# Sliding-window attention backward: scores and their gradients as 32-row products, and background work in smaller pieces

## The chip, the cores and the metric

One core of a Trainium2 chip runs one program. The metric is device time of one execution in microseconds (us). Engines are named as the profile names them: PE is TensorE (PEld its weight loads), DVE is VectorE, ACT is ScalarE, POOL is GpSimd, SP issues most DMAs.

## What is computed

The forward is a gate between an attention block and a ReGLU block, and the kernel returns the output and the gradients to x and to all weights:

```
x = A_x                                     # 2048 x 512, bf16
g = sigmoid((x * gate_w).sum(-1))
q, k, v = split(x @ wqkv)                   # 32 heads of 16 channels
p = softmax(q k^T / 4, masked to 0 <= i - j < 256)
a = (p v) @ wo
b = (relu(x @ W_gate) * (x @ W_up)) @ W_down
out = g * a + (1 - g) * b
return out, vjp(out)(grad_out)              # to x, wqkv, wo, W_gate, W_up, W_down, gate_w
```

For the attention part this means, for every head, the scores S = k q^T, the exponentials P, the product dP = v dO^T, P*dP, and from P and P*dP the outputs and the gradients to q, k, v.

## The kernel before, in words

The work has three stages. The first (lines 189 to 456) does the ReGLU forward and its gradients. The second, the **attention stage** (lines 458 to 918), is where the change lies. The third (lines 920 on) is a loop over 16 row tiles that makes the output and the gradient to x.

**Channels and heads.** The 512 channels are cut into four chunks `c` of 128 channels, which are 8 heads. A chunk is four strips of 32 channels, and a strip holds two heads. Tokens are cut into 16 blocks of 128. A *group* is a chunk and 512 tokens (`tg`); `project_parts` (line 119) makes for a group Q, dO, K, V in transposed form (128 channels x 512 tokens), four accumulated products of 128x512 each (function `mm`), a DMA transpose of Q and dO (`tr_rows`) and a PE transpose of K and V (`tr_kv`). K and V are also kept in two masked copies, K0/K1 and V0/V1 (lines 153 to 160): `par` (line 440) zeroes the second or the first head of every strip.

**Units.** The attention stage is a list of 360 *units* (lines 627 to 641). A unit is a chunk, a query block `j`, a key block `kb` (j, j-1 or j-2; roles "d", "m" and "f") and a `half`, and it covers four of the eight heads: one from each strip. The loop from line 821 gives each unit one step `n`, and interleaves the stages of several units in it:

- `front` (643): one product `ST` of 128 rows by 512 columns. Its moving operand is `zt`, in which Q is spread out as a block diagonal: strip k stands in rows 32k to 32k+31 and columns 128k to 128k+127, and the rest is zero. Then exp on ACT to bf16 (`Pu`, or the first half of `PP`), and a triangular mask on POOL for roles "d" and "f".
- `front_dp` (663), at the end of the step: the like product `dPT` of V and the spread dO. `gradp` (671), one step later: P*dP on DVE. The spreading is done by four DMAs a group (`spread`, line 468); for the first group by copies (lines 145 to 151).
- `flip`: P and P*dP transposed, for later use as stationary operands; for units marked `dma` by a DMA transpose at step n+2, for the others at step n+3 by 8 PE transposes into PSUM (`pt`) and a copy out by ACT and DVE in turn.
- `rowsum` (679), at step n+3: 8 small products into `BA`. `small_ops` follow on DVE and POOL once for each j. `cd_piece` (480): 8 small products into `CD`.
- Background work: the parts of the next group's projection (`prq`), each part in one piece, and the weight gradients of the chunk before (`bgq`, `grad_parts`, line 557) in pieces of four products. A `credit` (lines 872 to 897) with fixed costs decides in which steps a piece goes out; while a piece with more to come is held open, no projection starts.

**PSUM**, eight banks: tag M has four one-bank buffers, shared by `ST`, `dPT`, projections and weight gradients; TR has two, for transposes; `CD` and `BA` have one each.

All engines run in the order in which the program issues to them, with semaphores between them. `manual_schedule` means that the order is the written one.

Of the kernel before, what the change touches and what calls it, by code (L numbers as in the profile page):

```python
# [22 lines left out]
def kernel(  # L23
# [89 lines left out]
    if True:  # L113
# [5 lines left out]
        def project_parts(c, tg):  # L119
# [3 lines left out]

            def mm(nm, which, eng):
                ps, tag, bufs, _ = pools["now"]
                pp = ps.tile([P, TGW], F32, tag=tag, bufs=bufs, name="pp")
                for cd in range(DC):
                    if which < 3:
                        nc.tensor.matmul(pp[:], lhsT=w_p[c][:, cd, which * P:(which + 1) * P], rhs=x_T[tg][:, cd, :],  # L129
                                         start=(cd == 0), stop=(cd == DC - 1))  # L130
                    else:
                        nc.tensor.matmul(pp[:], lhsT=w_p[c][:, cd, 3 * P:4 * P], rhs=da_T[tg][:, cd, :],
                                         start=(cd == 0), stop=(cd == DC - 1))
                if nm in ("Q", "dO"):
                    if nm == "Q":
                        t4["z"] = pjA.tile([P, 2, TGW], BF, tag="zT", name="zT")
                    dst = t4["z"][:, ("Q", "dO").index(nm), :]
                else:
                    dst = pjA.tile([P, TGW], BF, tag="T", bufs=2, name=f"{nm}T")[:]
# [5 lines left out]
                if nm in ("Q", "dO"):  # L145
                    if c == 0 and tg == 0:
                        w = ("Q", "dO").index(nm)
                        for k in range(NP):
                            rows = slice(32 * k, 32 * k + 32)
                            evac(zt[0][rows, w, :, k, :], dst[rows, :].rearrange("p (k q) -> p k q", k=TPG),  # L150
                                 (("dve", "act")[w] if k % 2 else "dve"))
                else:
# [9 lines left out]
            def tr(a_nm, b_nm):  # L162
                ps, tag, bufs, trt = pools["now"]
                pt = ps.tile([P, 2, TPG, P], BF, tag=trt, bufs=2, name="ptp")
                for a, nm in enumerate((a_nm, b_nm)):
                    for k in range(TPG):
                        nc.tensor.transpose(pt[:, a, k, :], t4[nm][:, k * P:(k + 1) * P], ident[:])
                return pt
# [7 lines left out]
            def tr_kv():  # L176
# [9 lines left out]
            return [lambda: mm("Q", 0, "dve"), lambda: mm("dO", 3, "dve"), tr_rows, lambda: mm("K", 1, "act"),  # L186
                    lambda: mm("V", 2, "act"), tr_kv]

    with ExitStack() as p1, tc.manual_schedule():
# [210 lines left out]
        pools["now"] = (ps1, "tr", 2, "tr")  # L400
# [3 lines left out]
        for n in range(N1 + 8):  # L404
# [38 lines left out]
            if t in (NT + 3, NT + 5):  # L443
                i = (t - NT - 3) // 2
                nc.gpsimd.memset(zt[i][:, 0, :, :, :], 0.0)
                nc.vector.memset(zt[i][:, 1, :, :, :], 0.0)
            if n == N1 - 2:
                first = project_parts(*groups[0])
            for _ in range({N1 + 1: 2, N1 + 2: 0}.get(n, 1)):
                if first:  # L450
                    first.pop(0)()
# [7 lines left out]
    if True:  # L459
# [7 lines left out]
        pools["now"] = (ps, "M", 4, "TR")  # L467
        def spread(gi, k):
            rows = slice(32 * k, 32 * k + 32)
            nc.sync.dma_start(zt[gi % ZB][rows, :, :, k, :],  # L470
                              proj[groups[gi]]["z"][rows, :, :].rearrange("p w (k q) -> p w k q", k=TPG))

# [7 lines left out]
        def cd_piece(c, kb, qb, half, last):  # L480
# [5 lines left out]
            for hh in range(HH):  # L486
                h = 2 * hh + half
# [52 lines left out]
        def load_wo():  # L540
            t = pjA.tile([P, 2, TGW], BF, tag="zT", name="wo_z")
# [15 lines left out]
        def grad_parts(c, rest=None):  # L557
# [13 lines left out]
            hold = {}  # L571

# [7 lines left out]
            def piece(part, t0, first, last):  # L580
                if first:
                    tag, bufs = ("TR", 2) if part == DC and rest is not None else ("M", 4)
                    hold[part] = ps.tile([P, 3, P] if part < DC else [P, D], F32, tag=tag, bufs=bufs, name="wps")
                wps = hold[part]
                for t in range(t0, t0 + 4):
                    go_, no_ = first and t == t0, last and t == t0 + 3
                    if part < DC:
                        nc.tensor.matmul(wps[:], lhsT=x_r[:, t, part * P:(part + 1) * P], rhs=sts[c][:, t, 0:3, :],  # L588
                                         start=go_, stop=no_)
                    else:  # L590
                        nc.tensor.matmul(wps[:], lhsT=sts[c][:, t, 3, :], rhs=rows[t], start=go_, stop=no_)
                if not last:
                    return None
                if part < DC:
                    ws = (gwp if rest is None else S2["t6"]).tile([P, 3, P], BF, tag="ws", bufs=2 if rest is None else 5, name="ws")
                    evac(ws[:], wps[:], "act" if rest is None or part % 2 else "dve")
                    return store(part, ws)
                if t0 + 4 < NT:
                    hold["half"] = gwp.tile([P, D], F32, tag="half", bufs=1, name="half")
                    evac(hold["half"][:], wps[:], "act")  # L600
# [4 lines left out]
                if "half" in hold:  # L605
                    nc.vector.tensor_tensor(out=ws[:], in0=hold["half"][:], in1=wps[:], op=ALU.add)
                else:
                    evac(ws[:], wps[:], "act")
# [10 lines left out]
            for part, a, b in parts:  # L619
                for t0 in range(a, b, 4):  # L620
                    out.append((lambda part=part, t0=t0, f=(t0 == a), l=(t0 + 4 == b): piece(part, t0, f, l), t0 + 4 < b))
# [6 lines left out]
        for c in range(DC):  # L628
            for j in range(NT):
                kbs = [k for k in (j - 1, j, j - 2) if k >= 0]  # L630
                for half in range(2):
                    order = kbs if half or len(kbs) < 3 else [kbs[0], kbs[2], kbs[1]]
                    for ki, kb in enumerate(order):
                        u = Unit()
                        u.c, u.j, u.kb, u.half = c, j, kb, half
                        u.first = ki == 0 and half == 0
                        u.last = ki == len(kbs) - 1 and half == 1
                        u.role = ("d", "m", "f")[j - kb]
                        u.dma = (u.role == "d" or (u.role == "m" and half == 0 and j % 2 == 1)) and (c < DC - 1 or j < NT - 2)
                        units.append(u)  # L640
        NU = len(units)

        def front(u):
            tg, jl = u.j // TPG, u.j % TPG
            z = zt[(u.c * NTG + tg) % ZB]
            KTt = proj[(u.c, u.kb // TPG)][f"K{u.half}"]
            ksl = slice((u.kb % TPG) * P, (u.kb % TPG + 1) * P)
            ST = ps.tile([P, HH, P], F32, tag="M", bufs=4, name="ST")
            nc.tensor.matmul(ST[:], lhsT=KTt[:, ksl], rhs=z[:, 0, jl, :, :], start=True, stop=True)  # L649
# [5 lines left out]
            nc.scalar.activation(u.Pu[:], ST[:], ACT.Exp)  # L655
# [7 lines left out]
        def front_dp(u):  # L663
            tg, jl = u.j // TPG, u.j % TPG
            z = zt[(u.c * NTG + tg) % ZB]
            VTt = proj[(u.c, u.kb // TPG)][f"V{u.half}"]
            ksl = slice((u.kb % TPG) * P, (u.kb % TPG + 1) * P)
            u.dPT = ps.tile([P, HH, P], F32, tag="M", bufs=4, name="dPT")
            nc.tensor.matmul(u.dPT[:], lhsT=VTt[:, ksl], rhs=z[:, 1, jl, :, :], start=True, stop=True)  # L669

        def gradp(u):
            if u.role != "d" and not u.dma:
                u.Pd = wk.tile([P, HH, P], BF, tag="Pd", bufs=3, name="Pd")
            nc.vector.tensor_tensor(out=u.Pd[:], in0=u.Pu[:], in1=u.dPT[:], op=ALU.mult)  # L674

        def rowsum(u):
# [4 lines left out]
            for hh in range(HH):  # L681
                h = 2 * hh + u.half
# [11 lines left out]
        def flip(u):  # L694
# [8 lines left out]
            pt = ps.tile([P, 2, HH, P], BF, tag="TR", name="pt")  # L703
# [96 lines left out]
        with tc.manual_schedule():  # L800
            ev = {}
            cdq = []
            bgq = []
            prq = []
            credit = 1.2
            SLOT = 1.5
            LAG = 3
            n = 0

# [3 lines left out]

            def background():
                f, more = bgq.pop(0)
                store = f()
                if store is not None:
                    ev.setdefault(n + 2, []).append(("dma", store))
                return more

            while n <= NU + LAG or ev or cdq or bgq:
# [5 lines left out]
                if u is not None:  # L827
# [3 lines left out]
                    if u.first and u.j % TPG == 0:  # L831
                        if gi + 1 < len(groups):
                            prq = project_parts(*groups[gi + 1])
                            due = n + sum(2 * min(3, j + 1) for j in range(u.j, u.j + TPG)) - 3
                            if gi + 2 == len(groups):
                                due -= 10
# [4 lines left out]
                    if u.first and u.j == TPG - 1 and u.c > 0:  # L841
                        bgq += ready
# [27 lines left out]
                if u is not None:  # L870
                    front_dp(u)
                credit += SLOT - 0.63 - (0.44 if LAG <= n < NU + LAG and not units[n - LAG].dma else 0.0)
                for _ in range(2 if len(cdq) > 6 or (len(cdq) > 1 and cdq[1][5] and cdq[1][0] <= n and cdq[1][2] < NT - 1) else 1):
                    if cdq and cdq[0][0] <= n:
                        cd_piece(*cdq.pop(0)[1:])
                        credit -= 0.2
                if n >= NU:
                    if bgq:
# [5 lines left out]
                elif held and credit > 0.3:  # L884
                    held = background()
                    credit -= 0.65
                elif prq and not held and (credit > 0.4 or due - n <= len(prq)):
                    credit -= (0.44, 0.86, 0.86, 0.1, 0.86, 0.86)[len(prq) - 1]
                    prq.pop(0)()
# [138 lines left out]
```

## Time and profile before

| | us |
|---|---|
| three runs, median (lowest to highest) | 970.55 (968.0 to 971.43) |
| profiled execution, its own time | 971.04 |
| its span in the profile | 969.0 |
| first and last start of `ST` (line 649) | 259.0 and 772.9 |
| PE busy, whole span | 938.9 |
| DVE, ACT, POOL busy, whole span | 501.5, 473.8, 488.4 |

The granted clock of the profiled execution was 0.994 on average. The attention stage lies between the two starts in the table: 513.9 us, or 1.43 us for one of the 360 units. "Busy" of PE is to be read with care: a matmul's row lasts until its modelled end, and the next one starts long before that. What a matmul costs PE is therefore the distance from its start to the next start, not the length of its row.

### The profile page before, as it was taken

The numbers are of one execution on the slowest core, as the hardware profiler recorded it, in microseconds if no ns is written. First come the engines' busy times: TensorE is split into PE (matmuls) and PEld (weight loads), VectorE is DVE, ScalarE is ACT, GpSimd is POOL, SyncE is SP. The second block draws the span as 40 slices with busy tenths as digits, with TensorE's granted clock in tenths as the row PEclk, the third lists the DMA queues.
The fourth block names the chain that finished last, engine by engine and source line by source line (L and its number), as shares of the span: only waits on it lengthen the run. The fifth ranks groups of instructions, "written<-read, shape, count | busy, mean of one in ns | idle before, by whom it ended". The sixth has DMA issues, their size and how long they took to land.

```text
span 969.0 us, 27638 instructions
## 1 busy us (share of the span) xinstructions
PE 938.9 (97%) x11281; PEld 598.3 (62%) x11281; DVE 501.5 (52%) x918; ACT 473.8 (49%) x811; POOL 488.4 (50%) x936
## 2 busy tenths in 40 slices
PE   7999999999999999999999999989999999999998
PEld 4556555656567777676776677756777754444443
DVE  4443323323377777666776667765667613223322
ACT  5422322222378777667776667766677720001001
POOL 2644345444177667666676556665657622121211
PEclk9999999999999999999999999998999999999999
DMA  9988899996667598985889857899999969866760
GB/s 291 185 201 206 218 218 210 220 196 174 143 114 122 100 160 155 154 146 100 145 126 189 138 103 139 127 162 175 160 141 229 185 184 260 194 171 165 183 155 28
DMA packets 447415, 161.64 MB, mean 167 GB/s; under 512 B 365784, under 2 KB 444984, under 8 KB 447288
## 3 DMA queue, kind: packets, MB, share of 16 engines
q1 hardware_dynamic: 424888, 136.80, 73.8%
q10 hardware_dynamic: 20592, 17.84, 6.1%
q0 software_dynamic: 1808, 5.24, 1.5%
q8 instruction: 88, 1.44, 0.7%
q14 instruction: 39, 0.32, 0.1%
HBM read 38.44 MB, written 38.41 MB: 79 GB/s over the span
## 4 chain that ended last, share of the span: by engine, by line
PE 82%; DMA 6%; POOL 4%; SPq 2%; DVE 2%; ACT 1%; issue 1%; ACTq 0%; POOLq 0%; DVEq 0%
PE pt L706 9%; PE dxps L970 8%; PE ST L649 7%; PE dPT L669 7%; PE wps L373 6%; PE wps L588 4%; PE dxps L991 4%; PE BA L683 4%; PE pp L129 4%; PE bps L941 4%; PE CD L488 4%; PE dhps L326 3%; PE ups L326 3%; PE dps L375 3%; PE gps L326 3%; PE CD L491 2%
## 5 line engine op out<-in xcount | busy, mean ns | idle before, releaser
L674 DVE TENSOR_TENSOR Pd<-Pu,dPT 128x512 bf16<-128x512 bf16 x201 | 136.6, 681 | 64.9 <-POOL Pu L660 53.5
L655 ACT ACTIVATE Pu<-ST 128x512 bf16<-128x512 f32 x201 | 121.6, 606 | 58.9 <-PE ST L649 57.3
L649 PE MATMUL ST<-z,K 128*128 128x512 bf16 x360 | 136.8, 380 | 4.0 <-DVE Pd L674 1.7
L669 PE MATMUL dPT<-z,V 128*128 128x512 bf16 x360 | 137.2, 381 | 1.3 <-DVE Pd L674 1.1
L674 DVE TENSOR_TENSOR PP<-PP,dPT 128x512 bf16<-128x512 bf16 x159 | 108.4, 682 | 41.0 <-POOL PP L657 38.1
L657 POOL TENSOR_SCALAR_AFFINE_SELECT PP<-PP 128x512 bf16<-128x512 bf16 x128 | 81.3, 635 | 79.5 <-ACT PP L655 78.8
L655 ACT ACTIVATE PP<-ST 128x512 bf16<-128x512 f32 x159 | 95.7, 602 | 51.7 <-PE ST L649 42.0
L340 POOL TENSOR_TENSOR hT<-rg,upm 128x512 bf16<-128x512 bf16 x44 | 52.2, 1186 | 123.9 <-DVE upm L338 98.4
L488 PE MATMUL CD<-rq,p 128*128 128x32 bf16 x1440 | 109.7, 177 | 0.8 <-ACT rows_st L494 0.5
L373 PE MATMUL wps<-dgu_r,x_r 128*128 128x256 bf16 x704 | 105.6, 272 | 4.9 <-DVE wst L74 4.9
L491 PEld LDWEIGHTS <-p 128*128 128x128 bf16 x1440 | 86.4, 96 | 35.9 <-issue 3.1
L72 ACT COPY p<-pt 128x1024 bf16<-128x1024 bf16 x103 | 105.1, 1020 | 5.2 <-PE pt L706 2.5
L491 PE MATMUL CD<-rq,p 128*128 128x16 bf16 x1440 | 106.7, 169 | 0.0
L488 PEld LDWEIGHTS <-p 128*128 128x128 bf16 x1440 | 99.0, 96 | 1.7 <-issue 1.5
L660 POOL TENSOR_SCALAR_AFFINE_SELECT Pu<-Pu 128x512 bf16<-128x512 bf16 x112 | 71.0, 634 | 41.8 <-ACT Pu L655 40.1
L373 PEld LDWEIGHTS <-x_r 128*128 128x128 bf16 x704 | 68.8, 98 | 36.7 <-issue 6.3
L948 ACT COPY a_sb<-aps 128x512 f32<-128x512 f32 x16 | 9.4, 585 | 145.8 <-issue 133.1
L706 PE MATMUL pt<-ident,Pd 128*128 128x128 bf16 x804 | 78.4, 220 | 0.0
L706 PE MATMUL pt<-ident,Pu 128*128 128x128 bf16 x804 | 77.7, 219 | 0.0
L74 DVE COPY p<-pt 128x1024 bf16<-128x1024 bf16 x102 | 69.5, 681 | 6.1 <-PE pt L706 5.4
L332 ACT ACTIVATE rg<-gps 128x512 bf16<-128x512 f32 x44 | 26.3, 598 | 91.0 <-PE gps L326 49.6
L683 PE MATMUL BA<-KV,Pu 128*128 128x33 bf16 x804 | 66.6, 178 | 4.1 <-ACT BAs L689 4.0
(158 smaller groups left out, 1998.7 us busy)
## 6 DMA issues: line engine op xcount, KB each, us to landing
dqkvo_d<-rows_st SPq DMA_DIRECT2D x7, 1024.0 KB, 5.7
dar<-da_d SPq DMA_DIRECT2D x28, 256.0 KB, 4.3
hT_d<-hT ACTq DMA_DIRECT2D x44, 128.0 KB, 2.4
dgT_d<-dgu ACTq DMA_DIRECT2D x44, 128.0 KB, 2.8
duT_d<-dgu ACTq DMA_DIRECT2D x44, 128.0 KB, 2.8
duT_g<-duT_d SPq DMA_DIRECT2D x8, 640.0 KB, 5.2
dgT_g<-dgT_d SPq DMA_DIRECT2D x7, 640.0 KB, 9.1
gt<-hT_d SPq DMA_DIRECT2D x7, 640.0 KB, 5.7
```

The costliest lines, as they stand in the source:

```text
L72: nc.scalar.copy(out, in_)
L326: nc.tensor.matmul(out[:], lhsT=w(c), rhs=x(c), start=(c == 0), stop=(c == DC - 1))
L373: nc.tensor.matmul(acc["w"][:, c, :], lhsT=x_r[:, t, c * P:(c + 1) * P], rhs=k.dgu_r[:, :, i, :], start=(go_ and c % 2 == 0), stop=no_, sk ...
L488: nc.tensor.matmul(cd[0][:, h, :], lhsT=p2[:, 0, hh, :], rhs=rq[:, h, 0:2 * Dh], start=cd[1], stop=True, skip_group_check=True)
L491: nc.tensor.matmul(cd[0][:, h, 0:Dh], lhsT=p2[:, 1, hh, :], rhs=rq[:, h, 2 * Dh:3 * Dh], start=False, stop=True, skip_group_check=True)
L649: nc.tensor.matmul(ST[:], lhsT=KTt[:, ksl], rhs=z[:, 0, jl, :, :], start=True, stop=True)
L655: nc.scalar.activation(u.Pu[:], ST[:], ACT.Exp)
L657: nc.gpsimd.affine_select(out=u.Pu[:], in_=u.Pu[:], compare_op=ALU.is_ge, fill=0.0, base=0, pattern=[[0, HH], [1, P]], channel_multiplier=-1)
L669: nc.tensor.matmul(u.dPT[:], lhsT=VTt[:, ksl], rhs=z[:, 1, jl, :, :], start=True, stop=True)
L674: nc.vector.tensor_tensor(out=u.Pd[:], in0=u.Pu[:], in1=u.dPT[:], op=ALU.mult)
L683: nc.tensor.matmul(BA[:, h, 0:33], lhsT=u.Pu[:, hh, :], rhs=kv[:, u.kb % TPG, h, 1:34], start=(u.first and hh == 0), stop=True, skip_group ...
L706: nc.tensor.transpose(pt[:, a, hh, :], src[:, hh, :], ident[:])
```

## The change

- A unit now covers two strips, both heads of each: `half` selects strips 0 and 1 or strips 2 and 3, and the six units of a query block are listed so that `half` alternates.
- `ST` and `dPT` become a tile `SD` of two banks. Each of the two products of 128x512 becomes four products with 32 rows (one strip, masked to one head) and 128 columns. `products(u, v)` issues at the start of step n the scores of unit n and the dP of unit n-1, eight products, in the order V0 V0 K0 K0 V1 V1 K1 K1. Because `half` alternates, the four of one round lie on four different strips and in four different banks.
- The spread copies of Q and dO, their DMAs (60), the first group's copies and the clearing of `zt` go away; the products read Q and dO as projected.
- PSUM: M has two buffers of two banks, for `SD` alone while units run. Projections and weight gradients move to tag "tr", which has two buffers and is shared with the transposes of `flip`.
- Projections go out in halves of two products, weight gradients in pieces of two. One list `bg` holds both; a budget spreads its cost evenly over the steps up to the end of the group (`until`), with planned costs of a step in `base`. The weight gradients of a chunk come in three lots.
- In the last chunk the last four query blocks (before: two) flip on PE alone, and so do three of the first units; 213 units flip on PE, before 205.

```diff
+            def mm_part(nm, which, cds):
+                if 0 in cds:
+                    ps, tag, bufs = pools["now"]
+                    acc4[nm] = ps.tile([P, TGW], F32, tag=tag, bufs=bufs, name="pp")
+                src = x_T[tg] if which < 3 else da_T[tg]
+                for cd in cds:
+                    nc.tensor.matmul(acc4[nm][:], lhsT=w_p[c][:, cd, which * P:(which + 1) * P], rhs=src[:, cd, :],
+                                     start=(cd == 0), stop=(cd == DC - 1))
...
-                if nm in ("Q", "dO"):
-                    if c == 0 and tg == 0:
-                        w = ("Q", "dO").index(nm)
-                        for k in range(NP):
-                            rows = slice(32 * k, 32 * k + 32)
-                            evac(zt[0][rows, w, :, k, :], dst[rows, :].rearrange("p (k q) -> p k q", k=TPG),
-                                 (("dve", "act")[w] if k % 2 else "dve"))
...
+            for nm, which, eng in (("Q", 0, "dve"), ("dO", 3, "dve"), ("K", 1, "act"), ("V", 2, "act")):
+                out.append((0.432, lambda nm=nm, which=which: mm_part(nm, which, range(DC // 2)), True))
+                out.append((0.432, lambda nm=nm, which=which, eng=eng: mm(nm, which, eng), False))
+            out.insert(4, (0.0, tr_rows, False))
+            out.append((0.45, tr_kv, False))
...
-        pools["now"] = (ps, "M", 4, "TR")
-        def spread(gi, k):
-            rows = slice(32 * k, 32 * k + 32)
-            nc.sync.dma_start(zt[gi % ZB][rows, :, :, k, :],
-                              proj[groups[gi]]["z"][rows, :, :].rearrange("p w (k q) -> p w k q", k=TPG))
+        pools["now"] = (ps, "tr", 2)
...
+            step = 2 if rest is None else 4
...
+                elif first:
+                    hold[part] = ps.tile([P, 3, P] if part < DC else [P, D], F32, tag="tr", bufs=2, name="wps")[:]
...
+                order = [(j - 1, 0), (j - 2, 1), (j, 0), (j - 1, 1), (j - 2, 0), (j, 1)]
...
+                    u.dma = (u.role == "d" or (u.role == "m" and half == 0 and j % 2 == 1)) and (c < DC - 1 or j < NT - 4)
+                    if c == 0 and j < 2 and half == 0:
+                        u.dma = False
...
+        def score(u, nm, w, at, par):
+            tg, jl = u.j // TPG, u.j % TPG
+            lhs = proj[(u.c, u.kb // TPG)][f"{nm}{par}"]
+            z = proj[(u.c, tg)]["z"]
+            ksl = slice((u.kb % TPG) * P, (u.kb % TPG + 1) * P)
+            return [lambda i=i: nc.tensor.matmul(u.SD[:, i, at + par, :], lhsT=lhs[32 * (2 * u.half + i):32 * (2 * u.half + i) + 32, ksl],
+                                                 rhs=z[32 * (2 * u.half + i):32 * (2 * u.half + i) + 32, w, jl * P:(jl + 1) * P],
+                                                 start=True, stop=True, skip_group_check=True) for i in range(2)]
+
+        def products(u, v):
+            if u is not None:
+                u.SD = ps.tile([P, 2, 4, P], F32, tag="M", bufs=2, name="SD")
+            for par in range(2):
+                for f in (score(v, "V", 1, 2, par) if v is not None else []) + (score(u, "K", 0, 0, par) if u is not None else []):
+                    f()
...
-            nc.tensor.matmul(ST[:], lhsT=KTt[:, ksl], rhs=z[:, 0, jl, :, :], start=True, stop=True)
...
-            nc.scalar.activation(u.Pu[:], ST[:], ACT.Exp)
+            nc.scalar.activation(u.Pu[:].rearrange("p (i r) q -> p i (r q)", i=2), u.SD[:, :, 0:2, :].rearrange("p i r q -> p i (r q)"), ACT.Exp)
...
-            nc.tensor.matmul(u.dPT[:], lhsT=VTt[:, ksl], rhs=z[:, 1, jl, :, :], start=True, stop=True)
...
-            nc.vector.tensor_tensor(out=u.Pd[:], in0=u.Pu[:], in1=u.dPT[:], op=ALU.mult)
+            flat = lambda a: a.rearrange("p (i r) q -> p i (r q)", i=2)
+            nc.vector.tensor_tensor(out=flat(u.Pd[:]), in0=flat(u.Pu[:]), in1=u.SD[:, :, 2:4, :].rearrange("p i r q -> p i (r q)"), op=ALU.mult)
...
+            pt = ps.tile([P, 2, HH, P], BF, tag="tr", bufs=2, name="pt")
...
+            def base(m):
+                b = 0.205
+                if m <= NU:
+                    b += 0.33
+                if LAG <= m < NU + LAG:
+                    b += 0.205 if units[m - LAG].dma else 0.65
+                return b
...
+                        until = n + sum(2 * min(3, j + 1) for j in range(u.j, u.j + TPG)) - 3
+                        if u.j == TPG and u.c > 0:
+                            jobs = ready
+                        for _ in range((0, 2, 2, 2)[u.j // TPG] if u.c < DC - 1 else (0, 3, 3, 0)[u.j // TPG]):
+                            if jobs:
+                                bg += jobs.pop(0)
...
+                if n <= NU:
+                    products(u, units[n - 1] if n >= 1 else None)
...
+                elif bg:
+                    left = max(1, until - n)
+                    credit += (sum(base(m) for m in range(n, n + left)) + sum(b[0] for b in bg)) / left - base(n)
+                    while bg and credit >= 0.5 * bg[0][0]:
+                        credit -= bg[0][0]
+                        held = background()
+                    credit = max(-1.0, min(1.0, credit))
```

## The prediction, as put on record before the changed kernel ran

> **What bounds the kernel now.** I read the page's busy shares first, then busy time by stretches, then the timeline of a few steps.
>
> ```profile
> PE 938.9 (97%) x11281; PEld 598.3 (62%) x11281; DVE 501.5 (52%) x918; ACT 473.8 (49%) x811; POOL 488.4 (50%) x936
> ...
> L649 PE MATMUL ST<-z,K 128*128 128x512 bf16 x360 | 136.8, 380 | 4.0 <-DVE Pd L674 1.7
> L669 PE MATMUL dPT<-z,V 128*128 128x512 bf16 x360 | 137.2, 381 | 1.3 <-DVE Pd L674 1.1
> ```
>
> PE is always busy, and its `ST` and `dPT` hardly ever waited (4.0 and 1.3 us). But busy is row length, so I take prices from distances between starts:
>
> ```profile
> 500.36 0.38 PE L669 MATMUL dPT<-z,V 128*128 128x512 bf16 x1
> ...
> 500.57 0.18 PE L488 MATMUL CD<-rq,p 128*128 128x32 bf16 x1
> ...
> 500.60 0.17 PE L491 MATMUL CD<-rq,p 128*128 128x16 bf16 x1
> ...
> 502.24 0.38 PE L706 MATMUL pt<-ident,Pu 128*128 128x128 bf16 x4
> ...
> 502.46 0.39 PE L706 MATMUL pt<-ident,Pd 128*128 128x128 bf16 x4
> ```
>
> A 512-column product costs 0.21 us (500.36 to 500.57), though its row is 0.38 long; a 16- or 32-column one with its own weights 0.0256 (500.57 to 500.60; the 16 of two CD pieces elsewhere take 0.41); a 128-column one 0.055 (four in 0.22). A 384-column one is taken in proportion, 0.16.
>
> The attention stage by these prices, with the counts of the built program: ST and dPT 720 x 0.2133 = 154; BA and CD 5760 x 0.0256 = 147; flips 1640 x 0.0548 = 90; projections 240 x 0.2133 plus 7 of transposes = 58; weight gradients of three chunks 192 x 0.16 + 48 x 0.2133 = 41. Sum 490 of the 514 us between the first and the last ST. **The stage is bound by PE's issue**; 24 us are gaps, most of them BA behind the copy of the former BA on ACT, and starts of chunks. From the starts of ST, chunks last 118, 129, 128 and 139 us; the first is shorter, as it has no weight gradients beside it.
>
> The next limit shows in one unit, whose ST started at 501.82:
>
> ```profile
> 502.26 0.60 ACT L655 ACTIVATE PP<-ST 128x512 bf16<-128x512 f32 x1
> ...
> 502.94 0.63 POOL L657 TENSOR_SCALAR_AFFINE_SELECT PP<-PP 128x512 bf16<-128x512 bf16 x1 [0.32 <-ACT PP L655]
> ...
> 503.12 1.04 ACT L72 COPY p<-pt 128x1024 bf16<-128x1024 bf16 x1
> ...
> 503.60 0.69 DVE L674 TENSOR_TENSOR PP<-PP,dPT 128x512 bf16<-128x512 bf16 x1 [0.27 <-POOL PP L657]
> ```
>
> Scores to P*dP take 2.47 us (501.82 to 504.29), over two steps of 1.2 to 1.5. The four M buffers let PE run ahead of that. In full stretches ACT and DVE are busy some 75% (here, of 24 us):
>
> ```profile
> 331.00:355.00 24.00, 23.89 (x430) 17.18 (x428) 18.07 (x32) 17.95 (x31) 17.33 (x40) 1.00 0.90 161
> ```
>
> (PE, PEld, DVE, ACT, POOL, clock, share of DMA time, GB/s.)
>
> **The change, part by part.**
>
> *The eight products.* They replace 0.427 us a unit. No row shows 32-row products, nor four strips at once. From below: 8 x 0.0256 = 0.205, the rate of eight other products with eight weight loads (BA), if streaming is hidden wholly by overlap. From above: without overlap 8 x 0.0548 = 0.44; if besides PE has to empty at each change between 128-row and 32-row products, a short row lasts 0.170 where the next starts after 0.026, so 0.145 more, twice a step: 0.73. I take 0.32, the middle of the first two rows, since both are rows of 8 weight loads and 8 products, and only the overlap lies between them. Saving: 360 x (0.427 - 0.32) = 38 us of PE.
>
> The Trainium skill (TensorE: Matmul & The Clock Gate, Part 3: Packing small matmuls) gives 3.07 times for four 32-row products of 512 columns; by that a round of four would be about 0.07 us, an estimate, and the unit would stand at the bound from below. No run here shows it yet.
>
> *Flips.* Eight more on PE: 8 x 0.44 = 3.5 us. DMA transposes 155 to 147, and 60 spread DMAs of 64 KB less on SP's queue; nothing waits for SP at length, so nothing is gained (they would cost if DMA, at 0.5 to 1.1 of its time, were the bound; it gets lighter). Clearing `zt` (two memsets each on POOL and DVE) lay beside a full PE in the first stage: 0. ACT's exp and DVE's product keep 512 elements a partition: 0.6 and 0.68, as before.
>
> *New waits, first kind: "tr".* While a projection or a weight gradient is held open in one of the two "tr" buffers, two flips in following steps share the other. In the built order 69 of 210 steps with a flip wait so, 39 for an ACT copy, 30 for DVE. Timetable of such a pair, from the step's start: products to 0.32, BA 0.53, flip 0.97, its end seen at 1.2; ACT copies 1.2 to 2.22. The next flip would be due 0.53 into the next step, at 2.03 if this one lasted 1.5: it waits 0.25. Behind it on PE stand CD, the background piece and the next products. DVE copies 1.3 to 2.0: about no wait. Sum 39 x 0.25 = 10 us.
>
> *New waits, second kind: two SD buffers.* In the built program the first V product of a step waits for ACT (the exp of unit n-1, which reads the same tile), and the first K product for DVE (the P*dP of unit n-2). So PE can no longer run ahead. Two loops follow. Exp: 0.06 to see it + (0.32 - 0.04) issue + 0.22 for the last product + 0.06 + 0.60 = 1.22 a step. P*dP for a masked unit: 0.56 to exp + 0.60 + 0.08 + 0.635 + 0.06 + 0.68 + 0.06 less 0.08 (V goes ahead of K) = 2.6 for two steps; for role "m" 1.16 a step; over m, f, d on average 1.25. ACT's 1.02 us copies stand in both loops at times. So **a step can't be shorter than about 1.25**, whatever PE has to do.
>
> *Sum by chunk.* PE's work beside the products, from the built order, is 0.79 a step in chunk 0 and 0.98 in chunks 1 to 3 (0.96, 1.18 and 0.79 in the thirds of the last).
> - Chunk 0: 0.79 + 0.32 = 1.11, so the loops decide: 90 x 1.25 + 5 of gaps as before = 117, before 118: -1.
> - Chunks 1 and 2: (0.98 + 0.32) x 90 = 117, + 3 old gaps, + 3.5 tr waits, + 1.5 for short steps under 1.25: 125, before 129 and 128: -7 in all.
> - Chunk 3: thirds at 1.28, 1.50 and 1.25: 121, + 13 old gaps (start, clock at 0.86 for a while), + 2: 136, before 139: -3.
>
> Together -11, and 2 more where even spreading shortens the old waits of BA: **-13 us**. First and last stage are left alone. The profiled execution took 971.04 (span 969.0 and 2.0 around it), 0.5 above the median of the runs. **Forecast 958 us.** The gain of 38 on PE is mostly given back: 21 us of the stage becomes PE waiting for ACT and DVE.
>
> **Rivals.**
> 1. *Full overlap.* Products at 0.205. For it: nothing but the issue rate of BA. The loops shrink to about 1.15 to 1.2. Chunk 0 113, 1 and 2 118 each, 3 129: -36, **935 us**.
> 2. *No overlap.* Products at 0.44; the strips don't help. For it: the transposes' rows. The exp loop becomes 1.34, chunks 126, 134, 134, 144: +24, **995 us**. This is the change not doing what it says.
> 3. *PE empties at each change of form (the slower side).* Two changes a step at 0.145, with full overlap inside: 0.205 + 0.29 = 0.495. Steps: 0.9 + 0.495 = 1.4 in chunk 0, 1.47 in chunks 1 and 2, thirds of 1.45, 1.68 and 1.4. Chunks 131, 138.5, 138.5, 151: +45, **1016 us**; with products one by one besides, +130. It decides against the change from about 0.36 a unit on, that is 0.08 a switch. For it: rows of 0.17 with a next start after 0.026 show how much is in flight. Against it: nothing in this trace, which holds one form only.
>    The Trainium skill (TensorEngine Tiling (Array Packing), Key Properties) says it outright: "Changing tiling mode (not just tile) drains the TensorE". It states no price; no run shown so far has a change of mode.
> 4. *Loops longer than I think.* Products at 0.32, but ACT's copies (1.02, some 107) push exp back 0.2 to 0.35 each in most cases: +25 on my sum, **983 us**. For it: ACT and DVE at 75%, and PE without its lead. Against it: such a push hurts only where the step is short, and the budget fills steps evenly.
>
> **How the numbers follow.** Forecast case 0.42, rival 1 0.20, rival 2 0.12, rival 3 0.16, rival 4 0.10. The forecast case runs from about 940 to 972, so some of it is no change or a little slower. A measurement of this kernel can tell 0.3% (3 us) from no change. Faster: 0.20 + 0.35 = 0.55; within 0.3%: 0.05; slower: 0.02 + 0.38 = 0.40. Range: from 925 (rival 1 with shorter loops) to 1020 (rival 3), leaving out a tenth on each side. Of the faster cases alone, 928 to 965.
>
> **What would show it.** In the changed profile: the distance from the first V product to the first BA of a step is the price of the products (0.32; 0.2 and 0.44 to 0.5 for the rivals); if PE empties, the gap stands before the first V and before the first BA, with no releaser named. PE's idle time should now name ACT (exp) before V and DVE (P*dP) before K, and flips should wait for copies `p<-pt`. Steps of chunk 0 should be near 1.25 us. I am wrong if the products cost under 0.25 or over 0.4, or if steps are far from the longer of PE's work and 1.25.

## The result, and the profile after

The changed kernel takes **1012.08 us** (median of 4 runs, 1009.82 to 1013.17) against 970.99 for the kernel before: a ratio of 1.0427, 95% interval 1.0397 to 1.0456. It is 4.3% slower; the forecast was 958. The profiled execution took 1013.17, with a span of 1011.2, 42.2 more than before (969.0).

First the place: busy time over the attention stage, of the kernel before and of the changed one (the columns are the stretch, its length, busy us of PE, PEld, DVE, ACT and POOL, granted clock, share of DMA time, GB/s).

```profile
259.00:773.00 514.00, 500.27 (x8527) 356.46 (x8528) 354.15 (x644) 367.19 (x628) 333.45 (x772) 0.99 0.84 145
```

```profile
262.00:813.00 551.00, 492.70 (x10671) 357.13 (x10744) 365.48 (x648) 373.17 (x632) 336.78 (x771) 0.96 0.77 128
...
382.00:430.00 48.00, 42.17 (x924) 30.61 (x927) 33.09 (x60) 32.51 (x56) 32.54 (x77) 0.89 0.80 118
430.00:502.00 72.00, 64.87 (x1400) 46.02 (x1409) 45.91 (x82) 47.95 (x83) 42.40 (x95) 1.00 0.85 142
```

The stage is 37 us longer (first to last score product 261.9 to 813.0, before 259.0 to 772.9); the other 5 lie ahead of it and behind it. PE is busy 89% of it in place of 97% (a little more in truth: the page has 126 fewer rows of PE than of its weight loads). DVE has 11 us more to do and ACT 6, which fills neither, and the clock has fallen.

Then the products. PE's rows of one step in the changed kernel's timeline:

```profile
499.97 0.23 PE L649 MATMUL SD<-zT,V 32*128 32x128 bf16 x2
499.98 0.23 PE L649 MATMUL SD<-zT,K 32*128 32x128 bf16 x2
500.04 0.22 PE L649 MATMUL SD<-zT,V 32*128 32x128 bf16 x2
500.04 0.22 PE L649 MATMUL SD<-zT,K 32*128 32x128 bf16 x2
500.19 0.19 PE L687 MATMUL BA<-KV,PP 128*128 128x33 bf16 x1
```

Four products on four strips start within 0.01 us, the second round 0.07 later, and BA 0.15 after that. Before the first V, PE's start is later than the price of the product ahead of it by 0.076 (median, behind CD) or 0.10 (behind a projection). Sum **0.31 us** a step, where 0.427 stood. So PE's own work on these products did shrink, by 42 us.

What grew is shown by the page's groups (idle time before them, and what ended it, at the end):

```profile
L678 DVE TENSOR_TENSOR Pd<-Pu,SD 128x512 bf16<-128x512 bf16 x203 | 139.1, 685 | 71.2 <-PE SD L649 46.9
L666 ACT ACTIVATE Pu<-SD 128x512 bf16<-128x512 f32 x203 | 121.8, 600 | 88.6 <-PE SD L649 83.6
L649 PE MATMUL SD<-zT,V 32*128 32x128 bf16 x1440 | 120.4, 225 | 27.4 <-ACT PP L666 19.5
...
L649 PE MATMUL SD<-zT,K 32*128 32x128 bf16 x1440 | 105.2, 223 | 19.1 <-DVE PP L678 10.9
```

V waits for ACT, K waits for DVE, and ACT and DVE in turn wait for PE (`SD`): a ring, in which everybody waits for somebody and nobody is full. The page counts idle time only from the modelled end of the last row; from the start and the price of the last product (and 0.08 for the change of form) I count **33 us in which V waits for an exp that ended later, and 38.5 in which K waits for P*dP**. In about 170 of the 360 steps PE waits over 0.05 us for one of them or for both. One such wait in the changed kernel's timeline:

```profile
349.81 0.59 DVE L157 TENSOR_SCALAR V<-VT,par 128x512 bf16<-128x512 bf16 x1
...
350.04 0.23 PE L649 MATMUL SD<-zT,V 32*128 32x128 bf16 x2
350.33 0.68 DVE L678 TENSOR_TENSOR PP<-PP,SD 128x512 bf16<-128x512 bf16 x1
...
351.06 0.23 PE L649 MATMUL SD<-zT,K 32*128 32x128 bf16 x2 [0.79 <-DVE PP L678]
```

DVE is in the masked copies of a projection when P*dP falls due, PE has issued two V products and stands for a microsecond: the scores of unit n need the buffer that P*dP of unit n-2 still reads.

### The profile page after: what moved, and what is told of

Same layout as the page of the kernel before. It is cut to its first block, busy times and chain, and to the rows that moved or that the text cites. A ratio compares the mean times of both kernels' runs of the same rounds, so it can differ in the third digit from the quotient of the medians.

```text
span 1011.2 us, 31916 instructions
## 1 busy us (share of the span) xinstructions
PE 932.8 (92%) x13379; PEld 601.3 (59%) x13505; DVE 508.6 (50%) x914; ACT 478.7 (47%) x813; POOL 488.9 (48%) x934
## 5 line engine op out<-in xcount | busy, mean ns | idle before, releaser
L678 DVE TENSOR_TENSOR Pd<-Pu,SD 128x512 bf16<-128x512 bf16 x203 | 139.1, 685 | 71.2 <-PE SD L649 46.9
L666 ACT ACTIVATE Pu<-SD 128x512 bf16<-128x512 f32 x203 | 121.8, 600 | 88.6 <-PE SD L649 83.6
L649 PE MATMUL SD<-zT,V 32*128 32x128 bf16 x1440 | 120.4, 225 | 27.4 <-ACT PP L666 19.5
L678 DVE TENSOR_TENSOR PP<-PP,SD 128x512 bf16<-128x512 bf16 x157 | 107.5, 685 | 68.4 <-POOL PP L668 46.4
L649 PE MATMUL SD<-zT,K 32*128 32x128 bf16 x1440 | 105.2, 223 | 19.1 <-DVE PP L678 10.9
L649 PEld LDWEIGHTS <-V 32*128 32x128 bf16 x1440 | 56.8, 92 | 101.3 <-issue 92.9
L666 ACT ACTIVATE PP<-SD 128x512 bf16<-128x512 f32 x157 | 94.5, 602 | 46.0 <-PE SD L649 44.3
L481 PEld LDWEIGHTS <-p 128*128 128x128 bf16 x1440 | 94.0, 97 | 0.3
L484 PEld LDWEIGHTS <-p 128*128 128x128 bf16 x1440 | 87.4, 97 | 0.8 <-issue 0.5
L710 PE MATMUL pt<-ident,Pu 128*128 128x128 bf16 x812 | 81.4, 225 | 4.1 <-ACT p L72 2.3
L710 PE MATMUL pt<-ident,Pd 128*128 128x128 bf16 x812 | 82.7, 227 | 0.0
```

Of the source, the lines that this page charges most:

```text
L481: nc.tensor.matmul(cd[0][:, h, :], lhsT=p2[:, 0, hh, :], rhs=rq[:, h, 0:2 * Dh], start=cd[1], stop=True, skip_group_check=True)
L484: nc.tensor.matmul(cd[0][:, h, 0:Dh], lhsT=p2[:, 1, hh, :], rhs=rq[:, h, 2 * Dh:3 * Dh], start=False, stop=True, skip_group_check=True)
L649: return [lambda i=i: nc.tensor.matmul(u.SD[:, i, at + par, :], lhsT=lhs[32 * (2 * u.half + i):32 * (2 * u.half + i) + 32, ksl], rhs=z[32 ...
L666: nc.scalar.activation(u.Pu[:].rearrange("p (i r) q -> p i (r q)", i=2), u.SD[:, :, 0:2, :].rearrange("p i r q -> p i (r q)"), ACT.Exp)
L678: nc.vector.tensor_tensor(out=flat(u.Pd[:]), in0=flat(u.Pu[:]), in1=u.SD[:, :, 2:4, :].rearrange("p i r q -> p i (r q)"), op=ALU.mult)
L710: nc.tensor.transpose(pt[:, a, hh, :], src[:, hh, :], ident[:])
```

## The experiments

Theory A: the loss is PE waiting in two loops (exp to V, P*dP to K), since each unit's S and dP tie up a pair of banks and there are two pairs. Theory B: the loss lies in what PE itself has to issue (narrow products, changes of form, small pieces, shared "tr" buffers).

Ratios are to the kernel before, which ran beside each experiment; there its medians were 968.1 to 968.5 us, and 970.99 beside the changed kernel. A difference in us between two of the other kernels is therefore good to about 3 us.

**Wide products back.** `ST` and `dPT`, the spread copies, units of one head from each strip and four one-bank M buffers as in the kernel before, in the changed kernel's loop (the lines on the products alone):

```diff
-            u.SD = ps.tile([P, 2, 4, P], F32, tag="M", bufs=2, name="SD")
...
+            ST = ps.tile([P, HH, P], F32, tag="M", bufs=4, name="ST")
+            nc.tensor.matmul(ST[:], lhsT=KTt[:, ksl], rhs=z[:, 0, jl, :, :], start=True, stop=True)
...
+            nc.tensor.matmul(u.dPT[:], lhsT=VTt[:, ksl], rhs=z[:, 1, jl, :, :], start=True, stop=True)
```

> Part alone: the products are the old 128-row, 512-column ones again (spread copies, four one-bank buffers, dP at the end of its step), while the small pieces, the even budget, the shared tr buffers and the new unit order stay. Theory A (the loss is PE waiting for exp and for P*dP, because the narrow products tie S and dP of a unit to one pair of banks and leave two such pairs): those waits go, PE runs ahead again, only the tr waits (10 us) and eight more flips (3.5 us) stay, less what even spreading saves: about 980 us, from 968 to 988. Theory B (the loss comes from the pieces, the tr buffers and the budget): stays at 1000 us or more.

Measured: 984.25 us (ratio to the kernel before 1.0164, 1.0135 to 1.0192), clock 0.998. As A says: some 28 of the 41 us came with the narrow products and their paired banks, though these products are cheaper for PE. In the trace the gap ahead of flips is 13.8 us and PE's waits for exp or P*dP are all but gone; the longest entries of PE's waits in the stage are:

```profile
PE BA L698 <- ACT BAs L704: 7.2, 16, 1.1
PE pt L721 <- DVE p L74: 3.2, 5, 1.2
PE pt L721 <- ACT p L72: 3.0, 10, 0.5
```

**All eight products of one unit.**

```diff
-                for f in (score(v, "V", 1, 2, par) if v is not None else []) + (score(u, "K", 0, 0, par) if u is not None else []):
+                for f in (score(u, "K", 0, 0, par) + score(u, "V", 1, 2, par)) if u is not None else []:
```

> The eight products of a step all belong to the same unit (K0 K0 V0 V0 K1 K1 V1 V1): dP no longer comes a step later, so no product waits for the exp of the unit before; only two strips overlap at a time, in two banks. Theory A: the 33 us in which V waited for exp vanish, the wait for P*dP (38 us) shrinks by about half, since role m ends 0.7 us sooner; inside the products PE pays some 0.08 a step more (29 us): 975 to 995 us. Theory B (PE's own price of the narrow products is what costs): dearer by those 29 us, 1030 to 1045 us.

Measured: 1038.76 us (1.0726, 1.0689 to 1.0764). A's range is missed by 44 us, and the time is B's. The trace shows both sides. V waits for no exp any more, as it should. But the four rounds of two (starts 350.67, 350.73, 350.78, 350.84, BA at 351.00) and their entry cost 0.42 a step, 38 us more in all than the changed kernel's 0.31; K's wait rises instead of halving, to about 46 us by the gaps ahead of the first product; and the clock is 0.946. From 1012, less 33 for V's wait, with 38 for the products and 8 for K's wait, that gives 1025 us. For the other 14 the clock is enough: the stage has the half clock for 109 us in place of 48, and the distances between PE's rows there exceed their full-clock prices by 31 us in place of 11. So this time doesn't decide between A and B: V's wait went as A says, the products became a third dearer, and the clock fell.

**Masks left out.** The two `affine_select` of `front` are dropped.

> Leaves out the triangular masks on POOL, so the weights of masked pairs are not zeroed; all else as in the changed kernel. Exp to P*dP gets about 0.75 us shorter for two units in three. Theory A with the loop through P*dP binding: K's waits (38 us) mostly go, 975 to 990 us. Theory A with the loop through exp binding: V's waits stay, 1000 to 1008 us. Theory B: 1012 us, unchanged.

Measured: 999.85 us (1.036, 1.030 to 1.0421; the four runs lie between 997.38 and 1009.44). K's wait falls from 38.5 to 28 us, V's stays at 33. The gain is 12 us by the medians and about 6 by the ratios, whose intervals overlap, so its size is uncertain. It lies at the edge of A's second answer: the loop through P*dP counts, but cutting 0.75 us from it frees only about a quarter of K's waits.

**All copies of flips on DVE.**

```diff
-            eng = ("act", "dve")[copier["i"] % 2]
+            eng = "dve"
```

> All 213 copies of flips go to DVE, where one takes 0.68 us in place of 1.01 on ACT. Theory A, exp loop: exp is no longer late behind a copy, V's waits fall from 33 to about 10 us, K's waits rise by less than that as DVE gets 73 us more: 990 to 1005 us. If P*dP is what binds, DVE's load makes it later: 1012 to 1030 us. Theory B: 1012 us.

Measured: 991.82 us (1.0249, 1.0213 to 1.0285), 20 us less than the changed kernel. V's wait falls from 33 to 17.5, K's rises from 38.5 to 43, the gap ahead of flips from 10 to 5.5. The trace's list of what PE waited for at the products (line 649) shows it:

```profile
  DVE PP L678: 10.7, 23
  ACT PP L666: 8.3, 24
  DVE Pd L678: 3.1, 9
  ACT Pu L666: 3.0, 12
```

(us, times; in the changed kernel ACT's two entries were 19.5 and 4.6.) Exp behind a copy of 1.01 us was about half of V's wait.

**The same two edits in the kernel before, as controls.**

> Control: the kernel before, with all copies of flips on DVE. In the changed kernel this edit took 20 us off. Theory A: before, PE ran ahead of exp, so a late exp cost nothing; 966 to 972 us, no change. If ACT's copies cost PE time in any order of the products, this gets faster by 10 us or more.

Measured: 974.24 us (1.0063, 1.0042 to 1.0084): 2 us above the range for no change and slightly slower, where the same line gave 20 us after the change.

> Control: the kernel before, leaving out the masks on POOL (masked pairs keep weights that are not zero). In the changed kernel this took 12 us off. Theory A: here PE doesn't wait for the masks, so 962 to 970 us, within 0.6% of the kernel before.

Measured: 964.73 us (0.9962, 0.9945 to 0.9979): 4 us, where it gave 6 to 12. So before the change PE was hardly waiting for these engines, and afterwards it is. The copies show this clearly, the masks less so.

**Both edits in the changed kernel.**

> The changed kernel with both: copies of flips on DVE, and the masks left out. If the two loops (exp to V, P*dP to K) are what is lost, the two gains add, 20 + 12: about 980 us, from 974 to 986, with V's and K's waits together under 45 us. If only the later of the two loops counts, 988 to 992 us.

Measured: 983.32 us (1.0158, 1.0121 to 1.0196), V's and K's waits together 51 us (15.5 and 35), where under 45 was expected. The gains nearly add, 29 us where the two alone gave 32. Even so K waits 35 us.

**Wide products, with transposes alone in "tr".** The run with wide products, with projections and weight gradients in M again:

```diff
-        pools["now"] = (ps, "tr", 2)
+        pools["now"] = (ps, "M", 4)
...
-                    hold[part] = ps.tile([P, 3, P] if part < DC else [P, D], F32, tag="tr", bufs=2, name="wps")[:]
+                    hold[part] = ps.tile([P, 3, P] if part < DC else [P, D], F32, tag="tr" if rest is not None else "M", bufs=2 if rest is not None else 4, name="wps")[:]
```

> As the run with wide products back, but projections and weight gradients take their PSUM from the four one-bank buffers of the products again, so that flips have the two tr buffers for themselves; small pieces and the even budget stay. If the 16 us by which that run stood above the kernel before came from flips waiting for a copy of the flip before (14 us of gaps between BA and the flip in its trace), this one is at 968 to 974 us. If it came from small pieces, the new order of units or the budget, it stays at 980 us or more.

Measured: 975.40 us (1.0064, 1.004 to 1.0088), just above the range. The shared buffers cost 9 of the 16 us. What the other 7 are (eight more flips on PE are 3.5) I didn't take apart; a gain from even spreading doesn't show.

**Two fillers a step.** In the changed kernel, with BA's tile made a whole bank wide:

```diff
+                if LAG <= n < NU and not units[n - LAG].last:
+                    for _ in range(2):
+                        nc.tensor.matmul(BAt["full"][:, 400:512], lhsT=ident[:], rhs=x_r[:, 0, 0:112],
+                                         start=False, stop=True, skip_group_check=True)
```

> The changed kernel with two products of 128 rows by 112 columns more at the end of nearly every step, whose results nobody reads (spare columns of BA's bank): 0.1 us a step of streaming, 33 us in all if none of it falls into a wait. It asks what the lower granted clock (0.972, in the stage 0.96) hangs on. Theory A, with the clock following how much PE streams: the clock rises to 0.985 or more, and since part of the fillers falls into waits for exp and P*dP, the time is 1005 to 1020 us. If the clock falls with the 32-row form itself, it stays near 0.97 and the time is 1020 to 1045 us.

Measured: 1009.38 us (1.0428, 1.0398 to 1.0458), so 28 us of useless products cost nothing. The clock is back, in the stage and in the stretch that had 0.89:

```profile
262.00:811.00 549.00, 510.97 (x11348) 379.65 (x11348) 364.00 (x647) 374.76 (x630) 337.53 (x773) 1.00 0.76 128
382.00:430.00 48.00, 43.66 (x992) 32.16 (x992) 33.73 (x61) 33.42 (x58) 31.98 (x76) 1.00 0.76 123
```

V's and K's waits fall to 24 and 30, so 17 of the 28 us went into waits. The higher clock paid for the other 11: the distances in half-clock stretches exceeded the full-clock prices by 11 us in the changed kernel, and by 1 here.

**Order without alternation.**

```diff
-                order = [(j - 1, 0), (j - 2, 1), (j, 0), (j - 1, 1), (j - 2, 0), (j, 1)]
+                order = [(j - 1, 0), (j, 0), (j - 2, 0), (j - 1, 1), (j, 1), (j - 2, 1)]
...
-                    order = [(j - 1, 0), (j - 1, 1), (j, 0), (j, 1)]
+                    order = [(j - 1, 0), (j, 0), (j - 1, 1), (j, 1)]
```

> The changed kernel with units in an order in which half does not alternate (j-1, j, j-2 of the first two strips, then of the others): in four steps of six, V and K of a step lie on the same two strips, so only two products overlap. It prices the overlap. The products should cost 0.08 to 0.11 us a step more there, as where all eight belonged to one unit: 1030 to 1045 us. If overlap of four is worth nothing, 1005 to 1015 us.

Measured: 1026.38 us (1.0618, 1.0578 to 1.0659), 14 us slower than the changed kernel and a little under the range. In the 232 steps where V and K share two strips, the eight products take 0.18 us from first to last (median), in place of 0.08. That would be 25 us; the distances inside the steps, K's waits with them, sum to only 18 more. The clock fell as well, to 0.965. The overlap of four strips is real and worth having; it only isn't what decides.

**The kernel before, with the first BA of a block later.**

```diff
-                    rowsum(w)
+                    if not (w.first and w.j > 0):
+                        rowsum(w)
...
+                if LAG <= n < NU + LAG and w.first and w.j > 0:
+                    rowsum(w)
```

(The second piece stands behind dP and CD.)

> The kernel before, with one thing moved: the first BA products of a query block, which wait for ACT's copy of the BA before, are issued after dP and CD of their step in place of ahead of them. The trace of the kernel before has 16.5 us of gaps between ST and BA. If PE's issue is what bounds that kernel, nearly all of the short ones (44, 0.15 to 0.5 us each) go: 955 to 963 us. If these gaps only hide other waits, no change, 966 to 970 us.

Measured: 964.80 us, 12 runs (0.9962, 0.9945 to 0.9979). It is faster than both kernels, but by 3.3 us of the 5 to 13 expected: gaps between ST and BA fall from 16.5 to 3.4 us, and others (ahead of dP, behind CD) take some of it back.

## Why the prediction was wrong

- **The bound before** (PE's issue): right, by the controls: the edits that give 20 and 6 to 12 us after the change give -6 and +4 before it. One reading was off: from the starts of `ST`, chunks of 90 units last 116, 131, 131 and 136 us, not 118, 129, 128 and 139. Their sum is the same.
- **Price of the products**: the size is right, and by luck. 0.32 was taken, as the middle between full overlap and none; 0.31 was measured: 0.08 inside, 0.15 from the second round to BA, 0.08 to 0.10 ahead. So the overlap is nearly full, two rounds of 0.07 and 0.055, which is less than the 0.205 taken as the bound from below. The rest is the change of form, which the forecast put at nothing. A round of four takes 0.07, as the estimate by the Trainium skill's factor of 3.07 (TensorE: Matmul & The Clock Gate, Part 3) had it. Rival 2 is out, and so is rival 1's price.
- **Rival 3** gave 1016 us, the closest time, and for the most part by luck: it named the right mechanism for the products, but the time was lost elsewhere. The trace shows a delay at each change of form. The Trainium skill (TensorEngine Tiling (Array Packing), Key Properties) says that such a change drains TensorE; the first V starts 0.10 us after a CD product whose row lasts 0.17, so that PE empties wholly isn't shown. Ahead of the first V the delay is 0.076 to 0.10, and the 0.15 behind the second round hold 0.055 of streaming, so about 0.095: some 0.17 a step for both, not 0.29.
- **Waits at "tr"**: right, 10 us predicted, 10.2 in the gaps ahead of flips; 7 of them end with an ACT copy, as the timetable had it, and 2 with a DVE copy, which it put at no wait.
- **"A step can't be shorter than about 1.25"**: this is the step that failed, with the sum built on it, in which a step costs the longer of PE's work and this floor. The chunks took 131, 140, 140 and 140 us, where the sum had 117, 125, 125 and 136. The steps of chunk 0, where PE has only 1.1 to do, took 1.43 to 1.48 (all: 1.53). In the changed kernel the scores of a unit lie 2.74 to 2.84 us ahead of the end of its P*dP, or 1.39 a step. That length holds PE's own waits too, so it is what the loop became and no bound by itself. Where my 2.6 went wrong: P*dP starts 0.21 to 0.33 after the mask, not 0.06, as DVE is in another instruction or dP has not come; exp to mask is 0.13 to 0.15, not 0.08. And role "m", booked at 1.16 a step, is hardly faster for having no mask: its P*dP starts 1.04 after exp, since dP comes only with the next step's products, which wait themselves. I priced each loop on idle engines; ACT and DVE are busy two thirds of the stage, and in the waits shown P*dP and exp stand behind another instruction there.
- **Short steps** got 1.5 us a chunk. But waits fall in single steps and are not made up for by long ones: chunk 0 lost 25 us in V's and K's waits, each of the others about 16; 71.5 us in all, of which my sum held about 20. Rival 4 named this mechanism and made it 25 where it was over 50.
- **The clock** was taken as given. It fell to 0.96 in the stage.
- **Sum by measured terms:** other PE work 340, products 112, V's and K's waits 71.5, tr 10: 533.5 of 551 us. Of the 17.5 left, 8 go when the fillers bring the clock back (480 of work with the fillers, 54 of waits, 7.5 at flips: 541.5 of 551). The distances in half-clock stretches put the clock's share at 11, so it is some 8 to 11 us. Most of the rest are gaps ahead of BA (7) and of the transposes of K and V (3.5), which stay with the fillers. Before: 490 of work, 24 of gaps. So 38 us less work ended in 37 us more time.

The limit behind it is PSUM. The Trainium skill (TensorEngine Tiling (Array Packing), Gotcha 1: PSUM Pressure) says that different row tiles write to different banks; no run here put two strips in one bank. In this kernel it means that eight products occupy four banks a step, so S and dP of a unit share a pair, and all that is left of running ahead is one unit. Before, four banks held four separate products. That the pairs, and not the narrow form itself, make PE wait rests on who ended its waits in the trace, on the run with all eight products of one unit, where V's wait for exp went, and on the runs with four one-bank buffers, where both waits went. No run took buffers away from the wide products. A version with a third pair of banks was not tried: the eight banks are full.

## What to carry to other kernels

A cheaper product can be worth less than nothing if its buffers shorten the lead of the engine that was the bound: count, before and after, how many units that engine can be ahead, and compare the loop's length as the trace has it, queues included, with the step. A loop's length is not the sum of its rows on idle engines: here 2.6 us by rows became 2.8 for a masked unit under load, and what counts is the latest of several loops in each step, not their mean. When an engine that was full becomes one of a ring, edits on the others that were worth nothing begin to pay, and added work on it can be free: here 17 of 28 us of fillers fell into waits, and the clock paid for the rest.

## What the runs showed of the hardware

The granted clock fell with the narrow products though PE never stood long: 0.994 before and 0.996 to 1.0 in the other runs with wide products, against 0.946 to 0.981 in six runs with narrow ones, and down to 0.72 in one stretch of 24 us:

```profile
766.00:790.00 24.00, 20.68 (x459) 17.70 (x459) 14.52 (x24) 15.73 (x27) 14.75 (x33) 0.72 1.15 228
```

In the traces' records the clock is only ever whole or half, in windows of 3.41 us; the lower figures are means over such windows. Two of them in a row, in the changed kernel:

```profile
286.15:292.97 6.82, 5.89 (x112) 4.46 (x111) 3.48 (x6) 4.48 (x9) 3.80 (x8) 0.50 0.32 60
```

PE's longest single gap at the products in the stage was 1.1 us. The Trainium skill (TensorE: Matmul & The Clock Gate, Part 1) ties the half clock to an idle window of about 3.4 us; no gap of that length is in this trace, and fillers of 0.1 us a step brought the clock back to 0.998 with most of the waits still there. So here the clock hung on how much PE streamed, not on unbroken idleness.

The traces also tell about how much. I cut the attention stage of each into its windows of 3.41 us and counted what PE streamed, at 0.417 ns for a moving column (512 in 0.2133 us), products that run side by side once. In ten traces (the six with wide products, and those with masks left out, copies on DVE, both edits, and fillers) the half clock follows 32 windows, which streamed 13 to 43%. Of 1442 windows after which the clock stayed whole, 9 streamed under 43%, the least 40%. PE's busy share by rows, 89% in the stage, doesn't show this. In the runs where two strips overlap, some windows with up to 50% were followed by the half clock, so this is a border for this mix of products and no rule. The changed kernel's own trace lacks rows and can't be counted like this.

Of a change of form, each way cost 0.08 to 0.10 us.
